# Attention and two expert layers on one core: cumulative logs moved to TensorE, k and q scaled by VectorE, the first expert's weights split during the last block, the last 512 tokens routed in one piece

## Chip, cores and metric

The kernel runs on one core of a Trainium2 chip. The metric is the device time of one execution in microseconds, median of several executions. Five engines work side by side, each through its own list of instructions in order: TensorE (PE, with PEld for its weight loads), VectorE (DVE), ScalarE (ACT), GpSimd (POOL), and SyncE (SP), which issues most transfers. An instruction waits for what it needs, and everything behind it on its engine waits too.

## Reference, cut to what matters

Three layers follow one another over 1536 tokens of 384 features.

```
for t in range(S):                       # gated linear attention, 2 x 8 heads, S=768, D=48
    state = f[t] * state + k[t] outer v[t]
    y[t] = q[t] @ state                  # f = sigmoid(f_logit)
h = x @ w_in                             # 384 -> 2048
g = h * tanh(softplus(h))
x = g @ w_out                            # 2048 -> 384
expert = argmax(x @ w_gate)              # 8 experts, up to 384 rows each, in token order
out = gate * (relu(x @ w1[e]) @ w2[e])   # 384 -> 1024 -> 384
```

## The kernel before

**Attention** is done in 12 chunks of 128 tokens (`chunk`). With c the running sum of log(1 + exp(-f_logit)) inside a chunk, k is multiplied by exp(c) and q by exp(-c), and matmuls do the rest. Steps of a chunk are named by its number: `e`, `l` (ACT, the logarithm), `sum` (DVE, the running sum, L575), `ek`, `eq` (ACT, the two exponentials, L582 and L585), `mk`, `mq` (POOL, the products, L589 and L591), `dd` (DVE, the chunk's whole decay, L593), `t`, `u`, `s`, `y` (PE: transposes of k, state update, scores, output), `sa` (DVE, the causal mask, L656), `d` (POOL, the decayed state, L637).

**The dense layer** goes in three blocks of 512 tokens and 16 groups of 128 hidden features: `H` (L757, 9 matmuls), the activation as a chain of ten instructions that alternate between ACT and DVE (L766, L773, L775, L770, L778, L780, L782, L784, L789, L792), and `A` (L801, 9 matmuls into three PSUM banks). Groups are counted 0 to 47, so H47 and A47 are the last. Products keep fp32 accuracy by splitting each operand into a high and a low part; the dense weights come packed and are decoded by ACT, DVE (L80, L82, L85) and POOL (L93) while the first block runs.

**Routing** (`copied`, `route`): after a block's last A the outputs are copied from PSUM (`xt`, L835, L837), logits taken (`lg`, L863), maximum and one-hot (`mx`, `oh`, L872, L877), positions counted (`pl`, `po`, L942 to L959), rows transposed (`tp`, L897) and scattered to DRAM. In the last block the first expert's rows do not go through DRAM: one-hot columns (`sel`, L982) and the split rows (`rh`, `rl`, L913, L915) go into matmuls (`mm`, L989) that add to the rows of earlier blocks (`d0`, L1017); their copies `0dh`, `0dl` are the input of expert 0.

**Experts** (`expert`, `expert_group`): each expert's weights are loaded in four pieces of 128 x 1536 and split by ACT and DVE in halves (`hi`, `lo`, L1064, L1066); expert 0 uses the memory of the dense layer's w_in, expert 1 that of w_out. Four hidden groups `EH` (L1147) and their second products `EA` (L1166) per expert follow; `tp`, `dh`, `dl` prepare the next expert's rows.

What runs when is decided by `Plan`: each step has an engine, a cost, a due time in units of groups and the steps it needs; a list scheduler turns that into one order, which is then fixed.

Of the kernel before, what the change touches and what calls it, by code (L numbers as in the profile page):

```python
# [34 lines left out]
class Kernel:  # L35
# [92 lines left out]
    def attention_scan(self, xg):  # L128
# [3 lines left out]
        with ExitStack() as ctx:  # L132
# [14 lines left out]
            for b in range(B):  # L147
                for g in range(H // 2):
                    tt = {}
                    for nm, src in (("q", self.q), ("k", self.k), ("f", self.f)):  # L150
                        t = tt[nm] = ld.tile([G, S], F32, tag="t" + nm, name="t" + nm)
                        for h in range(2):
                            nc.sync.dma_start(
                                out=t[h * D : (h + 1) * D, :].rearrange("p (c t) -> p c t", c=NC),
                                in_=src[b * NC : (b + 1) * NC, 64 * h : 64 * h + D, g, :].rearrange("c p t -> p c t"))
                    t = tt["f"]
# [255 lines left out]
class Plan:  # L412
# [4 lines left out]
    LAG = 80  # L417

# [9 lines left out]
    def order(self):  # L428
# [19 lines left out]
        while any(waiting.values()):  # L448
            for eng, w in waiting.items():
                if free[eng] > now:  # L450
                    continue
                for i, (_, _, s) in enumerate(w):
                    if not over(s["after"], now):
# [30 lines left out]
class Fast:  # L484
# [35 lines left out]
    def attention_setup(self):  # L520
        nc, pool = self.nc, self.work
        self.seg = pool.tile([128, H // 2, 128], F32, name="seg")
        nc.gpsimd.memset(self.seg, 1.0)
        nc.gpsimd.memset(self.seg[:, :, 0:1], 0.0)
# [16 lines left out]
    def chunk(self, n):  # L541
# [31 lines left out]
        def sums(_):  # L573
            T["cp"] = self.chunk_tile("cp", [128, H // 2, 128])
            nc.vector.tensor_tensor_scan(  # L575
                out=flat(T["cp"]), data0=flat(self.seg), data1=flat(T["f"]), initial=0.0, op0=ALU.mult, op1=ALU.add)
# [779 lines left out]
```

## Time and profile before

| | us |
|---|---|
| median of 3 executions | 497.9 (495.66 to 498.37) |
| the profiled execution: its own time | 500.67 |
| its span, first to last instruction | 498.9 |
| PE busy | 440.3 (88%) |
| DVE busy | 355.6 (71%) |
| ACT busy | 300.9 (60%) |
| POOL busy | 123.2 (25%) |
| mean granted TensorE clock (share of full) | 0.922 |

The busy share is a mean over stages that are limited by different engines, so the rows below are read by stage. An instruction's recorded time includes what it waits for after it has been started.

### The profile page before, as it was taken

How to read it: one execution, taken by the hardware profiler on the slowest of the kernel's cores; microseconds unless marked ns; L12 is line 12 of the kernel's file. 1: busy time of each engine (PE TensorE's matmuls, PEld its weight loads, DVE VectorE, ACT ScalarE, POOL GpSimd, SP SyncE). 2: the span in 40 equal slices, each digit the busy share in tenths (PEclk: the TensorE clock that was granted, in tenths of full speed). 3: DMA queues.
4: the chain of work that ended last, by engine and by line, in shares of the span. 5: the costliest groups of instructions: out<-in, count | busy, mean ns of one | idle time of the engine just before them, and what ended most of it. 6: DMA issues, size and time to landing. Idle time of an engine off the chain costs nothing.

```text
span 498.9 us, 7241 instructions
## 1 busy us (share of the span) xinstructions
PE 440.3 (88%) x2637; PEld 387.5 (78%) x2637; DVE 355.6 (71%) x590; ACT 300.9 (60%) x534; POOL 123.2 (25%) x114
## 2 busy tenths in 40 slices
PE   2964988894989999999999999577999999999992
PEld 2853776673768888888888888466999999999992
DVE  3889888999999975767787677976265475665310
ACT  5566587766577765557777777862274465556220
POOL 5688723325434221100001100004010121011011
PEclk9985778898999999999999999766899999999997
DMA  8765634444732001000600100464444865671000
GB/s 294 255 221 195 214 101 125 142 160 148 244 104 72 11 33 28 21 2 14 255 1 33 63 1 0 136 239 141 151 150 161 310 213 192 212 259 69 1 30 31
DMA packets 22047, 62.77 MB, mean 126 GB/s; under 512 B 3044, under 2 KB 10108, under 8 KB 22000
## 3 DMA queue, kind: packets, MB, share of 16 engines
q1 hardware_dynamic: 20208, 57.47, 34.7%
q0 software_dynamic: 1792, 4.73, 2.5%
q8 instruction: 23, 0.38, 0.3%
q14 instruction: 24, 0.20, 0.1%
HBM read 53.11 MB, written 8.68 MB: 124 GB/s over the span
## 4 chain that ended last, share of the span: by engine, by line
PE 41%; issue 28%; DVE 17%; DMA 6%; ACT 3%; POOL 2%; SPq 1%; POOLq 0%; DVEq 0%; ACTq 0%
PE bxp L801 16%; PE bhp L757 15%; DMA out_dram<-ys,rows 3%; DVE dec_t L85 3%; PE bat L670 2%; PE bat L675 2%; DVE dec_t L82 2%; PE bat L616 2%; PE bat L863 2%; DVE m_y L775 2%; PE bat L650 1%; DVE c_cp L575 1%; DVE dec_t L80 1%; DVE m_y L780 1%; DVE m_y L782 1%
## 5 line engine op out<-in xcount | busy, mean ns | idle before, releaser
L757 PE MATMUL bhp<-x,winh 128*128 128x512 f32 x288 | 90.9, 397 | 0.0
L757 PEld LDWEIGHTS bhp<-x,winh 128*128 128x128 f32 x288 | 54.1, 191 | 11.8 <-issue 0.6
L1156 DVE SCALAR_TENSOR_TENSOR gl<-bhp,gh 128x512 fp32r<-128x512 f32 x32 | 22.1, 690 | 56.9 <-ACT gh L1153 56.9
L1153 ACT ACTIVATE gh<-bhp 128x512 fp32r<-128x512 f32 x32 | 19.2, 600 | 66.2 <-PE bhp L1147 65.6
L757 PE MATMUL bhp<-x,winl 128*128 128x512 f32 x144 | 56.4, 392 | 0.0
L801 PE MATMUL bxp<-gh,wouth 128*128 128x512 f32 x144 | 45.7, 428 | 9.6 <-ACT gh L789 9.6
L1122 POOL DMA_INDIRECT out_dram<-ys,rows x16 | 16.4, 1024 | 127.6 <-ACT ys L1119 125.1
L969 POOL DMA_INDIRECT disp<-row,r_slot x12 | 14.5, 1208 | 131.6 <-ACT wouth L1064 58.0
L766 ACT ACTIVATE m_y<-bhp 128x512 f32<-128x512 f32 x48 | 28.6, 596 | 30.0 <-PE bhp L757 29.9
L801 PE MATMUL bxp<-gh,woutl 128*128 128x512 f32 x144 | 43.6, 413 | 0.0
L801 PE MATMUL bxp<-gl,wouth 128*128 128x512 f32 x144 | 43.4, 412 | 0.0
L780 DVE TENSOR_TENSOR m_y<-m_y,m_r 128x512 f32<-128x512 f32 x48 | 33.5, 699 | 11.4 <-ACT m_r L778 11.2
L770 ACT ACTIVATE m_r<-m_y 128x512 f32<-128x512 f32 x48 | 30.2, 630 | 17.2 <-DVE m_y L775 17.0
L792 DVE TENSOR_TENSOR gl<-bhp,gh 128x512 fp32r<-128x512 f32 x48 | 32.9, 686 | 9.8 <-ACT gh L789 9.3
L801 PEld LDWEIGHTS bxp<-gh,wouth 128*128 128x128 f32 x144 | 26.6, 199 | 16.7 <-ACT gh L789 11.8
L789 ACT ACTIVATE gh<-bhp 128x512 fp32r<-128x512 f32 x48 | 28.5, 594 | 13.6 <-DVE bhp L784 13.6
L782 DVE SCALAR_TENSOR_TENSOR m_y<-m_y,m_r 128x512 f32<-128x512 f32 x48 | 35.8, 748 | 0.8
L775 DVE TENSOR_SCALAR m_y<-m_y 128x512 f32<-128x512 f32 x48 | 26.0, 542 | 14.0 <-ACT m_y L773 13.6
L773 ACT ACTIVATE m_y<-m_y,root 128x512 f32<-128x512 f32 x48 | 34.7, 722 | 0.9
L801 PEld LDWEIGHTS bxp<-gl,wouth 128*128 128x128 f32 x144 | 29.0, 202 | 6.6
L801 PEld LDWEIGHTS bxp<-gh,woutl 128*128 128x128 f32 x144 | 28.9, 201 | 6.6
L1066 DVE TENSOR_TENSOR woutl<-raw,wouth 128x768 fp32r<-128x768 f32 x32 | 29.1, 953 | 6.5 <-ACT wouth L1064 6.3
(153 smaller groups left out, 1094.8 us busy)
## 6 DMA issues: line engine op xcount, KB each, us to landing
raw<-in_moe_w_dram SPq DMA_DIRECT2D x32, 768.0 KB, 5.1
stage<-in_moe_w_in_dram SPq DMA_DIRECT2D x8, 768.0 KB, 4.8
stage<-in_moe_w_out_dram SPq DMA_DIRECT2D x8, 768.0 KB
rows<-disp SPq DMA_DIRECT2D x9, 386.0 KB, 3.3
disp<-slot SPq DMA_DIRECT2D x1, 3088.0 KB, 11.1
c_f<-in_f_logit_dram SPq DMA_DIRECT2D x12, 256.0 KB, 3.9
c_k<-in_k_dram SPq DMA_DIRECT2D x12, 256.0 KB, 4.5
c_q<-in_q_dram SPq DMA_DIRECT2D x12, 256.0 KB, 3.7
```

The costliest lines, as they stand in the source:

```text
L757: nc.tensor.matmul(out=hp, lhsT=K.win[w][:, f // 2, kk, c], rhs=x[:, p, kk, :], start=(kk == 0 and n == 0), stop=(kk == KD - 1 and n == 2))
L766: nc.scalar.activation(out=T["y"], in_=T["h"], func=AF.Exp)
L770: nc.scalar.activation(out=T["r"], in_=T["y"], func=AF.Ln)
L773: add(f"{G}y2", "ACT", 740, G + .35, lambda _: nc.scalar.activation(out=T["y"], in_=T["y"], func=AF.Square, scale=ROOT, bias=K.root), [f"{ ...
L775: add(f"{G}y3", "DVE", 460, G + .4, lambda _: nc.vector.tensor_scalar(out=T["y"], in0=T["y"], scalar1=W_MAX, scalar2=0.5, op0=ALU.min, op1 ...
L780: add(f"{G}q1", "DVE", 740, G + .6, lambda _: nc.vector.tensor_tensor(out=T["y"], in0=T["y"], in1=T["r"], op=ALU.mult), [f"{G}r2"])
L782: add(f"{G}q2", "DVE", 740, G + .65, lambda _: nc.vector.scalar_tensor_tensor(out=T["y"], in0=T["y"], scalar=2.0, in1=T["r"], op0=ALU.subt ...
L789: nc.scalar.activation(out=T["g"][0], in_=T["h"], func=AF.Copy)
L792: add(f"{G}gl", "DVE", 700, G + .9, lambda _: nc.vector.tensor_tensor(out=T["g"][1], in0=T["h"], in1=T["g"][0].bitcast(F32), op=ALU.subtra ...
L801: nc.tensor.matmul(out=self.xa[kk][:, o], lhsT=K.wout[w][:, f, 128 * kk : 128 * (kk + 1)], rhs=T["g"][i][:, o], start=(f == 0 and n == 0), ...
L1066: nc.vector.tensor_tensor(out=lo[:, d], in0=r[:, s], in1=hi[:, d].bitcast(F32), op=ALU.subtract)
L1156: nc.vector.scalar_tensor_tensor(out=T["g"][1], in0=T["h"], scalar=0.0, in1=T["g"][0].bitcast(F32), op0=ALU.max, op1=ALU.subtract)
```

## The change

1. The running sum of a chunk is made by four matmuls with the causal matrix (`sum`, PE) instead of a scan on DVE. For that f_logit comes with tokens on the partitions. `ek`, `eq` and `dd` read it from PSUM; `dd` becomes an exponential on ACT.
2. `mk` and `mq` are done by DVE instead of POOL.
3. Expert 0's weights are split one half at a time when each part of w_in has been used for the last time, so during the last block. The last pieces wait for the activation of group 47. Expert 1's pieces wait until expert 0's rows are ready. The A of the last five groups is due one group later.
4. In the last block the four pieces of 128 tokens are routed together: one set of small instructions instead of two, with the row splits, gate weights and counts placed behind the one-hot columns.
5. `tp` of the experts is due later (u - .8 instead of u - 1.5), and the final check moves behind hidden group 2 of the experts.

```
-        add(f"{n}sum", "DVE", 700, u - 1, sums, [f"{n}l"], [(("cp",), [f"{n}mk", f"{n}mq", f"{n}dd"])])
+        def sums(taken):
+            T["lp"] = self.bank(taken[0])
+            for p in range(H // 2):
+                nc.tensor.matmul(
+                    out=T["lp"][:, 128 * p : 128 * (p + 1)], lhsT=T["f"][:, p, :], rhs=self.causal, start=True, stop=True)
+        add(f"{n}sum", "PE", 1050, u - 1, sums, [f"{n}l"], [(short[0], [f"{n}dd", f"{n}eq"])])
...
+        add(f"{n}dd", "ACT", 180, u - .75, whole, [f"{n}ek"])
-        add(f"{n}mk", "POOL", 1400, u - .6, lambda _: nc.gpsimd.tensor_tensor(
+        add(f"{n}mk", "DVE", 720, u - .6, lambda _: nc.vector.tensor_tensor(
             out=T["k"], in0=T["k"], in1=T["ek"], op=ALU.mult), [f"{n}ek", f"{n}k"])
-        add(f"{n}mq", "POOL", 1400, u - .5, lambda _: nc.gpsimd.tensor_tensor(
+        add(f"{n}mq", "DVE", 720, u - .5, lambda _: nc.vector.tensor_tensor(
             out=T["q"], in0=T["q"], in1=T["cp"], op=ALU.mult), [f"{n}eq", f"{n}q"])
...
-            add(f"A{G}{h}", "PE", 2040 if h == "" else 1080, G + self.LATE.get(h, 1.9), lambda _, o=o: across(_, o),
+            add(f"A{G}{h}", "PE", 2040 if h == "" else 1080, G + self.LATE.get(h, 2.1) + (G >= self.NG - 5), lambda _, o=o: across(_, o),
...
-        add(f"r{i}pl", "PE", 500, u + .1, place, [f"r{i}oh"] + ([f"r{i - 1}se"] if i else []), [(short, [f"r{i}po"])])
-        add(f"r{i}se", "DVE", 320, u + .2, seen, [f"r{i}pl"])
+        add(f"r{i}pl", "PE", 300 * count, u + .04, place, [f"r{i}oh"] + ([f"r{i - 1}se"] if i else []), [(short, [f"r{i}po"])])
+        add(f"r{i}se", "DVE", 160 * count, u + .4, seen, [f"r{i}pl"] + behind)
...
+        first = self.NG - NFB
+        def old(j):
+            G = first + 2 * j + 1
+            if e == 0:
+                return [f"H{G}"]
...
-            v = u - 4.5 + m + (.6 if m > 1 else 0)
+            v = u - 4.5 + m + (.6 if m > 1 else 0) if e else first + 4 * m + 4
...
+                add(f"{e}hi{m}{c}", "ACT", 850, v, lambda _, m=m, c=c: piece(m, c, True), [f"{e}raw{m}"] + old(2 * m + c) + (
+                    [f"0dl{KD - 1}"] if e == 1 else [f"{self.NG - 1}gl"] if e == 0 and m == 3 else []))
...
-                add(f"{e}tp{kk}", "PE", 260, u - 1.5, lambda taken, kk=kk: disp(kk, taken), [f"{e}rows"],
+                add(f"{e}tp{kk}", "PE", 260, u - .8, lambda taken, kk=kk: disp(kk, taken), [f"{e}rows"],
...
+        self.route(2 * self.NB - 2, self.NB - 1, 0, self.CPB, self.NG + .7, ("at", "xp0", "xp1", "xp2"))
```

Where the instructions stand is shown at three places, all on VectorE. First, the start of the program, from the first instruction of chunk 0; before the change:

```order
L575 SCALAR_TENSOR_TENSOR c_cp<-seg,c_f 128x512
L593 COPY dd<-c_cp 128x4
L575 SCALAR_TENSOR_TENSOR c_cp<-seg,c_f 128x512
L622 TENSOR_TENSOR c_st<-state_127,bat 128x384
L593 COPY dd<-c_cp 128x4
L656 TENSOR_TENSOR c_sa<-bat,causal 128x512
L656 TENSOR_TENSOR c_sa<-bhp,causal 128x512
```

The same place after it (L602 is `mk`, L604 `mq`, L667 the mask, L633 the state):

```order
L602 TENSOR_TENSOR c_k<-c_k,c_ek 128x512
L604 TENSOR_TENSOR c_q<-c_q,c_cp 128x512
L602 TENSOR_TENSOR c_k<-c_k,c_ek 128x512
L667 TENSOR_TENSOR c_sa<-bhp,causal 128x512 x2
L633 TENSOR_TENSOR c_st<-state_124,bhp 128x384
L604 TENSOR_TENSOR c_q<-c_q,c_cp 128x512
```

A scan and a small copy per chunk have gone; two products per chunk have come.

Second, VectorE while group 42 is in its activation, after the change (L786 to L803 are the activation, L1094 is the low half of a weight piece):

```order
L803 TENSOR_TENSOR gl<-bhp,gh 128x512
L791 TENSOR_TENSOR m_y<-m_y,m_r 128x512
L786 TENSOR_SCALAR m_y<-m_y 128x512
L793 SCALAR_TENSOR_TENSOR m_y<-m_y,m_r 128x512
L795 SCALAR_TENSOR_TENSOR bhp<-m_y,bhp 128x512
L791 TENSOR_TENSOR m_y<-m_y,m_r 128x512
L803 TENSOR_TENSOR gl<-bhp,gh 128x512
L793 SCALAR_TENSOR_TENSOR m_y<-m_y,m_r 128x512
L1094 TENSOR_TENSOR winl<-raw_2179,winh 128x768
L795 SCALAR_TENSOR_TENSOR bhp<-m_y,bhp 128x512
```

Six of the eight pieces now stand among the activations of groups 32 to 42 and two behind that of group 47; before, the first of the eight stood in that of group 46.

Third, VectorE from the copies of the last block's outputs on; before the change (L1066 is expert 1's weight split, L872 `mx`, L877 `oh`, L915 `rl`, L958 and L959 `po`):

```order
L835 COPY xt<-bxp_2317 128x256
L1066 TENSOR_TENSOR woutl<-raw_2866,wouth 128x768 x2
L872 TENSOR_REDUCE r_mx<-bat 128x2
L1066 TENSOR_TENSOR woutl<-raw_2883,wouth 128x768
L877 TENSOR_TENSOR r_oh<-bat,r_mx 128x16
L915 TENSOR_TENSOR rowl<-bat,rowh 128x384
L882 TENSOR_TENSOR r_ex<-bat,r_mx 128x16
L1066 TENSOR_TENSOR woutl<-raw_2883,wouth 128x768
L931 TENSOR_REDUCE r_sm<-r_ex 128x2
L932 TENSOR_SCALAR r_sm<-r_sm 128x2
```

After it (L897 `mx`, L902 `oh`, L941 `rl`, L986 and L987 `po`, L1012 `sel`):

```order
L855 COPY xt<-bxp_2360 128x256
L897 TENSOR_REDUCE r_mx<-bat 128x4
L902 TENSOR_TENSOR r_oh<-bat,r_mx 128x32
L941 TENSOR_TENSOR rowl<-bat,rowh 128x384
L941 TENSOR_TENSOR rowl<-bxp_2981,rowh 128x384
L941 TENSOR_TENSOR rowl<-bxp_2991,rowh 128x384
L986 TENSOR_TENSOR r_po<-r_oh,bxp_2996 128x32
L987 TENSOR_REDUCE r_slot_3023<-r_po 128x4
L1012 TENSOR_SCALAR sel<-iota_93,r_slot_3023 128x256
L941 TENSOR_TENSOR rowl<-bxp_3017,rowh 128x384
```

No weight piece stands in the routing any more, and there is one pass over four pieces of 128 tokens where there were two over two.

## Rows read from the trace of the kernel before

**Rows 1.** Three stages: engine busy us (instructions), granted clock, DMA share, GB/s

```profile
0.00:145.00 145.00, 108.26 (x633) 88.59 (x633) 128.34 (x172) 93.14 (x167) 77.90 (x68) 0.86 0.57 188
145.00:312.00 167.00, 165.95 (x892) 137.17 (x893) 127.50 (x248) 116.84 (x212) 23.03 (x26) 0.99 0.12 41
312.00:357.00 45.00, 33.13 (x169) 29.07 (x168) 30.10 (x73) 22.72 (x42) 5.84 (x5) 0.70 0.55 183
```

**Rows 2.** Groups by line, whole span: count | busy us, mean ns | idle before, releaser

```profile
L575 DVE TENSOR_TENSOR_SCAN c_cp<-seg,c_f 128x512 f32<-128x512 f32 x12 | 20.3, 1699 | 3.0 <-ACT c_f L568 3.0
L593 DVE COPY dd<-c_cp 128x4 f32<-128x4 f32 x12 | 4.9, 406 | 2.0 <-ACT c_cp L585 2.0
L85 DVE SCALAR_TENSOR_TENSOR dec_t<-stage,dec_t 128x768 int32<-128x768 int32 x16 | 22.0, 1376 | 0.0
L775 DVE TENSOR_SCALAR m_y<-m_y 128x512 f32<-128x512 f32 x48 | 26.0, 542 | 14.0 <-ACT m_y L773 13.6
L589 POOL TENSOR_TENSOR c_k<-c_k,c_ek 128x512 f32<-128x512 f32 x12 | 17.8, 1484 | 21.0 <-ACT c_ek L582 14.1 <-DVE m_y L782 3.5 <-DVE gl L792 2.9
L591 POOL TENSOR_TENSOR c_q<-c_q,c_cp 128x512 f32<-128x512 f32 x12 | 17.1, 1423 | 2.3 <-ACT c_cp L585 2.2
```

**Rows 3.** The same lines alone: duration ns min/median/max, first and last start

```profile
L575 DVE TENSOR_TENSOR_SCAN c_cp<-seg,c_f x12: 1208/1221/2868, 5.5 to 162.6; 128x512 f32<-128x512 f32 x12
L85 DVE SCALAR_TENSOR_TENSOR dec_t<-stage,dec_t x16: 944/954/2375, 17.4 to 139.6; 128x768 int32<-128x768 int32 x16
L775 DVE TENSOR_SCALAR m_y<-m_y x48: 412/427/2101, 60.8 to 316.1; 128x512 f32<-128x512 f32 x48
L780 DVE TENSOR_TENSOR m_y<-m_y,m_r x48: 674/684/1347, 64.6 to 319.7; 128x512 f32<-128x512 f32 x48
L784 DVE SCALAR_TENSOR_TENSOR bhp<-m_y,bhp x48: 668/690/697, 67.0 to 322.6; 128x512 f32<-128x512 f32 x48
```

**Rows 4.** What PE waited for, 20 to 145 us: total, times, longest

```profile
PE bat L600 <- POOL c_k L589: 7.3, 1, 7.3
```

**Rows 5.** The chain that ended last: start, us, what (slow and full clock)

```profile
52.73 2.05 PE bat L670 x8
227.00 0.89 PE bat L670 x8
```

**Rows 6.** Timeline of the dense layer's end: start, us, instruction, idle before

```profile
304.71 0.39 PE L757 MATMUL bhp<-x,winl 128*128 128x512 f32 x1
...
311.67 0.60 ACT L789 ACTIVATE gh<-bhp 128x512 fp32r<-128x512 f32 x1
...
312.87 0.39 PE L757 MATMUL bhp<-x,winl 128*128 128x512 f32 x1
...
323.99 1.65 PE L801 MATMUL bxp<-gh,wouth 128*128 128x512 f32 x3 [3.29 <-ACT gh L789]
...
326.71 1.48 PE L801 MATMUL bxp<-gl,wouth 128*128 128x512 f32 x3
```

**Rows 7.** What PE waited for, 312 to 360 us

```profile
PE bxp L801 <- ACT gh L789: 5.2, 2, 3.3
```

**Rows 8.** Timeline of the last block's routing up to expert 0

```profile
328.85 1.40 PE L863 MATMUL bat<-wg,xt 128*128 128x8 f32 x12
...
330.88 0.17 DVE L872 TENSOR_REDUCE r_mx<-bat 128x2 f32<-128x16 f32 x1
330.96 0.95 DVE L1066 TENSOR_TENSOR woutl<-raw,wouth 128x768 fp32r<-128x768 f32 x1
...
338.09 1.63 PE L989 MATMUL bhp<-sel,rowh 128*128 128x256 f32 x6
...
344.89 1.02 PE L989 MATMUL bhp<-sel,rowl 128*128 128x256 f32 x6
...
347.25 1.01 PE L1147 MATMUL bhp<-d,winh 128*128 128x256 f32 x3
```

**Rows 9.** Group by line: copy of an expert's rows on DVE

```profile
L1103 DVE TENSOR_TENSOR d<-bat,d 128x256 fp32r<-128x256 f32 x14 | 5.3, 415 | 0.0
```

More of the change, by code (lines that the diff above doesn't have):

```diff
@@ L451, in order @@
                     continue
+                soon = 1 << 60
                 for i, (_, _, s) in enumerate(w):
-                    if not over(s["after"], now):
+                    at = max([0] + [done.get(x, 1 << 60) for x in s["after"]])
+                    if at > now:
+                        soon = min(soon, at)
+                        continue
+                    if soon - now < self.PATIENCE * s["weight"]:
                         continue
@@ L852, in route @@
         last = b == self.NB - 1
         T = {}
-        u = NFB * (b + 1) + (1.5 + 3 * p if not last else .7 + p * .2)
-        xs = [f"{b}xt{kk}{p}" for kk in range(KD)]
-        short = ("at",) if not last else ("at", "hp")
-        def logits(taken):
-            lg = self.bank(taken[0])
-            for t in range(2):
-                o = 256 * p + 128 * t
+        ch = slice(p, p + count)
+        R = range(count)
+        small = lambda *x: self.route_small(b, *x)[:, ch]
+        behind = [f"r{i}sel{count - 1}"] if last else []
@@ L862, in logits @@
+        half = lambda t: [f"{b}xt{kk}{(p + t) // 2}" for kk in range(KD)]
+        def logits(t, taken):
+            if t == 0:
+                T["lgb"] = self.bank(taken[0])
+                T["lg"] = T["lgb"][:, : count * E].rearrange("p (t e) -> p t e", e=E)
+            for j in (t, t + 1):
+                o = 128 * (p + j)
                 for kk in range(KD):
                     nc.tensor.matmul(
-                        out=lg[:, E * t : E * (t + 1)], lhsT=self.xt[b][:, kk, o : o + 128],
+                        out=T["lg"][:, j], lhsT=self.xt[b][:, kk, o : o + 128],
@@ L915, in parts @@
                 nc.vector.tensor_tensor(out=T["rl"][:, t], in0=y, in1=T["rh"][:, t].bitcast(F32), op=ALU.subtract)
-        for t in range(2):
+        for t in R:
             ends = [f"r{i}row{t}"] + ([f"r{i}rl{t}"] if last else [])
-            add(f"r{i}tp{t}", "PE", 350, u + (.5 + .5 * t if not last else .05), lambda taken, t=t: rows(t, taken), xs + (
-                [f"r{i}tp0"] if t else []),
-                [(short, ends)] + ([(("row0" if b == 0 else "row",), [f"r{i}sc"])] if t == 0 else []))
+            add(f"r{i}tp{t}", "PE", 350, u + (.5 + .5 * t if not last else .05), lambda taken, t=t: rows(t, taken),
+                half(t) + ([f"r{i}tp{t - 1}"] if t else []) + ([f"r{i}pl"] if t == 3 else []),
+                [(short, ends)] + ([(("row0" if b == 0 else "row",), [f"r{i}sc{t // 2}"])] if t % 2 == 0 else []))
```

190 lines of the change are left out of this document (100 added, 90 removed).

## Prediction

> **What bounds the kernel now.** I read the busy time by stage first, because the share over the whole span (PE 88%) hides that three engines take turns. In the first 145 us VectorE is busy 128.3 us and PE only 108.3, at a granted clock of 0.86; from 145 to 312 PE is busy 166.0 of 167 us and nothing else matters; from 312 to 357 PE is busy 33.1 of 45 us at 0.70 of its clock [rows 1]. So a gain has to come out of VectorE before 145, and out of the waits between 312 and 357; in between, each microsecond put on PE is a microsecond lost.
>
> Next I asked why VectorE is so busy early. For single lines the view shows a median close to the minimum and a mean far above it: the scan 1221 ns median, 2868 at most, 1699 on average; the last decode step 954, 2375 and 1376; the clamp in the activation 427, 2101 and 542 [rows 2, 3]. The line L784, whose second input lies in PSUM, never goes beyond 697 ns [rows 3]. The excess of mean over median is 12 x 0.48 = 5.7 us for the scan, 16 x 0.42 = 6.8 for the decode step, 48 x 0.115 = 5.5 for the clamp: 18 us of VectorE's time in three lines is waiting, and almost all before 170 us, where GpSimd is busy 77.9 of 145 us [rows 1]. The products of k and q are 17.8 + 17.1 = 34.9 us of GpSimd's time [rows 2].
>
> By a rule of the Trainium skill ("SBUF — State Buffer", section "Who interferes with whom") a VectorE instruction with two SBUF inputs, or in a mode that uses both ports, and a GpSimd instruction that reads SBUF shut each other out for a whole instruction. The lines above agree. It also speaks against this change, see the second rival.
>
> Last the end of the dense layer. H45 ends at 305.10 and its high part `gh` at 312.27, so the activation takes 7.2 us up to the point where A can start. H47 ends at 313.26, but A47 starts only at 323.99 and ends at 328.19 [rows 6]: 10.7 us instead of 7.2, because expert 0's weight pieces stand between its instructions. PE waits for it twice, 5.2 us in all [rows 7]. From A47's end to expert 0's first matmul at 347.25 another 19.1 us pass; in them a weight piece of 0.95 us stands directly behind the first small routing instruction, and logits and matmuls run in two rounds [rows 8].
>
> **The change part by part.**
>
> *Scan, products and decay, up to 145 us.* VectorE loses 12 scans (20.3 us) and 12 small copies (4.9) [rows 2] and gets 24 products. The trace has no such product on VectorE; the nearest row is L780, the same shape with two SBUF inputs, at 684 ns [rows 3]: 16.4 us. Balance -8.8 us. On what stays, the waiting behind GpSimd should fall as GpSimd's work falls: 34.9 us go, nearly all of them early, out of some 85 to 90 that lie in the first 170 us (77.9 up to 145 [rows 1]), about 40%. Of the 12.3 us of excess in the decode step and the clamp that is -4.9. The new products will themselves wait sometimes: between 0 and what each scan waited, 24 x 0.48 = 11.5 us; L780's mean lies near its median, so I take 2. VectorE: -8.8 - 4.9 + 2 = about -12 us, bounds +3 (no relief, full waits) and -21 (all waits gone).
>
> How much of it reaches the end? PE has 36.7 us idle in this stage [rows 1] and must take the sums in. A sum is four matmuls of the shape of L670, whose eight records take 0.89 us at the upper clock level (2.4 GHz) and 2.05 us at the lower (1.2 GHz) [rows 5]. In the new order eight sums stand before group 12, some 8 to 16 us, hidden in idle time that is largely the very waiting for VectorE; one 7.3 us wait of PE for a product on GpSimd should go as well [rows 4]. PE gets tight, so I let 10 of the 12 us through: **-10** (bounds -18 and +3).
>
> *Four later sums.* They stand where PE is full: 4 x 0.89 = **+3.6**.
>
> *Expert 0's weights in the last block.* Six pieces of 0.95 us on VectorE [rows 8] and as many copies on ScalarE go among the activations of groups 32 to 42. Their cover is idle time: VectorE 127.5 and ScalarE 116.8 us busy of 167 [rows 1]. But latency counts too: `gh` of group 45 was ready 0.83 us before its A could start (312.27 against 313.10, the end of A44 and H47 as PE counts it) [rows 6]. A piece on each engine delays by up to 1.8 us, 1 us more than the slack. Bounds 0 and 6 x 1; I take **+1.5**.
>
> *End of the dense layer.* H47 comes one A earlier, since A44 to A47 stand behind it: -2.04, the time of an A as of an H (305.10 to 313.26 holds two of each). Without the pieces A47 can start 7.2 us after H47; three A fill 6.1 of them. It ends at about 7.2 + 2.3 = 9.5 us after H47, before it was 14.9: -5.4. What is late next is the copy of the outputs, not expert 0's weights: the two last pieces run beside A47. Together **-7.4** (bounds -9 and -5).
>
> *Routing in one piece.* From A47's end: copies up to the start of the logits 0.7 us (328.19 to 328.85); logits 1.4, one set of transposes 0.4 (three twelfths of the logits' 1.4), logits 1.4; maximum and one-hot, two of 0.17, 0.4 with their gaps; then PE's transposes and counts against VectorE's three row splits, which I put at 2.2 (three of three quarters of L780's 0.69, and 0.6 until the first can start); position and one `sel` 0.7, four times 0.17; 24 matmuls at the old 1.0 to 1.6 us for six, 5.2; and 1.3 from the last of them (345.91) to expert 0. That makes 13.7 against 19.1 us [rows 3, 8]. **-5.5** (bounds -8 at the upper clock, -3).
>
> *Expert 1's weights and the later `tp`.* Expert 1's pieces move out of the routing into expert 0, where VectorE is less than half busy; before the change the pieces of the following experts run there too. The next expert's row copies now have only two second products in front of them as cover, and in VectorE's order three pieces of 0.95 us stand among three copies of 0.42 [rows 8, 9]: 4.1 us against two products of about that length. **+0.5** (bounds 0 and 7 x 0.5).
>
> Sum: -10 + 3.6 + 1.5 - 7.4 - 5.5 + 0.5 = -17.3 us. The profiled execution took 500.67 us, its span 498.9; it would take 483.4. The median of the runs shown is 2.8 us lower, so I predict **480.5 us**.
>
> **The rivals.**
>
> *The early gain passes whole.* VectorE sheds its waits nearly completely and PE, less interrupted, keeps the upper clock: -18 in place of -10, 472.5 us. For it: PE's clock of 0.86 and 0.70 is low where it idles. Against: PE's extra sums in the same stage.
>
> *The products wait as the scans did.* GpSimd keeps the decode's low halves and the state updates; if every product waits 0.48 us and nothing else is relieved, VectorE gains nothing and the early term is 0: 490.5 us. By that rule of the Trainium skill each product, with two SBUF inputs, is exposed. Against: L780 has the same operands and a mean near its median, though most of it runs after GpSimd is done.
>
> *Routing gains half.* The chain of PE, ScalarE and VectorE in one piece has fewer overlaps than two rounds, and the clock stays low: -2.5 in place of -5.5, A47 -5 in place of -7.4: 486 us.
>
> *Slower.* PE takes its list in order, and a sum waits for ScalarE's logarithm; where that is late, groups queue behind it, as they did behind L600 for 7.3 us [rows 4]. There are 12 sums. To end more than 0.5% above the old time this would have to cost 17.3 + 2.5 = 19.8 us, or 1.65 us for each sum. Three waits like the one seen would do it. Against: PE has other work in front of most sums, and the logarithms are due a group ahead.
>
> **How the numbers follow.** The forecast with its own spread (476 to 485): 0.45. Whole early gain: 0.2. Waiting products: 0.15. Half the routing: 0.13. Slower: 0.03. The rest, 0.04, is a gain so small that it can't be told from none; about 0.5% is what a measurement of this kernel can tell. The range reaches from the better rival less 5 us (its bound of -21 us for VectorE and -8 for routing) to the waiting products: 467 to 491. Faster by over 0.5% (below 495.4) holds in all but the last two cases: 0.93; within 0.04; slower 0.03.
>
> **What would show it.** Right: the busy time of PE up to the point where it runs full shrinks in stretch, that point moves from 145 to 135 us or less, medians and means of the decode and clamp lines come together, the products stand near 0.69 us, from H47's end to expert 0's first matmul 23 us or less pass instead of 34. Wrong: the products show means near 1.2 us; PE waits for the logarithm in front of L580, or for `gh` in groups 33 to 43; PE waits for row copies between experts, which would show as idle time of up to 0.5 us before the first hidden group of each expert.

## Result and profile after the change

The changed kernel takes 482.2 us (479.68 to 483.49, 4 runs) where the kernel before takes 497.9 in the same comparison: ratio 0.969, 95% interval 0.964 to 0.974. A second comparison (below) gave 481.5 us and 0.965 (0.961 to 0.969). The profiled execution has a span of 480.5 us (before 498.9) and a mean granted clock of 0.951 (0.922). For one version below, "A later everywhere", time and ratio are from the four fast ones of its six executions, while its profile is of a slow one (492.5 us).

By stage, to be held against [rows 1]. The values are the stretch, its length, the busy us of PE, PEld, DVE, ACT and POOL (with instructions), the granted clock, the DMA share and GB/s. The first cut is where PE runs full; the last stretch holds more of the dense layer and of the experts than 312 to 357 us did before, so it is not the same work:

```profile
0.00:140.00 140.00, 112.62 (x704) 93.53 (x705) 117.08 (x172) 91.87 (x175) 47.04 (x48) 0.89 0.60 193
140.00:298.00 158.00, 157.68 (x875) 130.52 (x875) 120.36 (x241) 112.50 (x211) 14.61 (x20) 1.00 0.18 59
298.00:345.00 47.00, 44.41 (x263) 39.33 (x262) 32.35 (x65) 27.88 (x51) 4.63 (x4) 0.89 0.26 86
```

PE runs full from 140 us on (before: 146). Up to that point VectorE is busy 117.1 us in 172 instructions instead of 129.3 in 174 (before, cut at 146), PE 112.6 instead of 108.3, GpSimd 47.0 instead of 78.1.

The lines that waited behind GpSimd, and the new product, each alone (duration in ns, min/median/max), for [rows 3]:

```profile
L85 DVE SCALAR_TENSOR_TENSOR dec_t<-stage,dec_t x16: 940/945/1260, 20.8 to 134.8; 128x768 int32<-128x768 int32 x16
L786 DVE TENSOR_SCALAR m_y<-m_y x48: 408/426/1502, 57.6 to 309.7; 128x512 f32<-128x512 f32 x48
L602 DVE TENSOR_TENSOR c_k<-c_k,c_ek x12: 676/684/1626, 9.5 to 209.4; 128x512 f32<-128x512 f32 x12
```

and grouped over the whole span (busy us, mean ns), with the product of q (L604), for [rows 2]:

```profile
L786 DVE TENSOR_SCALAR m_y<-m_y 128x512 f32<-128x512 f32 x48 | 22.2, 462 | 9.6 <-ACT m_y L784 9.2
L85 DVE SCALAR_TENSOR_TENSOR dec_t<-stage,dec_t 128x768 int32<-128x768 int32 x16 | 15.4, 965 | 0.0
L604 DVE TENSOR_TENSOR c_q<-c_q,c_cp 128x512 f32<-128x512 f32 x12 | 9.8, 819 | 1.2 <-ACT c_cp L591 1.2
L602 DVE TENSOR_TENSOR c_k<-c_k,c_ek 128x512 f32<-128x512 f32 x12 | 9.4, 787 | 8.4 <-ACT c_ek L587 8.4
```

The mean of the decode step went from 1376 to 965 ns and now lies near its median of 945; the clamp's from 542 to 462, with a median of 426. The products take 787 and 819 ns on average, the one of k with a median of 684.

What PE waited for from 145 to 300 us, where the weight pieces of expert 0 now stand:

```profile
PE bxp L812 <- ACT gh L800: 0.3, 2, 0.2
```

The end of the dense layer and the routing, PE's timeline (L768 H, L812 A, L887 logits, L1018 `mm`, L1185 expert 0), for [rows 6, 8]:

```profile
307.02 0.39 PE L768 MATMUL bhp<-x,winl 128*128 128x512 f32 x1
...
314.84 0.96 PE L812 MATMUL bxp<-gh,wouth 128*128 128x512 f32 x3 [1.14 <-ACT gh L800]
...
316.33 0.86 PE L812 MATMUL bxp<-gl,wouth 128*128 128x512 f32 x3
317.02 0.82 PE L1046 MATMUL bhp<-ident,rows 128*128 128x128 f32 x6
317.68 1.40 PE L887 MATMUL bat<-wg,xt 128*128 128x8 f32 x12
...
324.12 1.01 PE L1018 MATMUL bhp<-sel,rowh 128*128 128x256 f32 x3
...
330.74 0.62 PE L1185 MATMUL bhp<-d,winh 128*128 128x256 f32 x3 [0.50 <-DVE d L1060]
```

H47 ends at 307.41, A47 starts 7.4 us later and ends at 317.19, expert 0 starts at 330.74: 23.3 us after H47 instead of 34.0. The nine matmuls of A47 stand in three lines of three (triples below). They take 0.96, 0.85 and 0.86 us where they took 1.65, 1.48 and 1.48 [rows 6]; the granted clock from A47's start to its end is 1.00 (2.4 GHz), before it was 0.50 (1.2 GHz). Before, PE waited 1.9 us ahead of A46 and 3.3 ahead of A47, and the lower level set in within A46; in the changed kernel PE waits once, 1.1 us. A46 before the change:

```profile
317.24 0.96 PE L801 MATMUL bxp<-gh,wouth 128*128 128x512 f32 x3 [1.94 <-ACT gh L789]
318.04 1.39 PE L801 MATMUL bxp<-gh,woutl 128*128 128x512 f32 x3
319.22 1.49 PE L801 MATMUL bxp<-gl,wouth 128*128 128x512 f32 x3
```

### The profile page after: what moved, and what is told of

Read it like the earlier page. It is cut to its first block, busy times and chain, and to the rows that moved or that the text cites. A ratio compares the mean times of both kernels' runs of the same rounds, so it can differ in the third digit from the quotient of the medians.

```text
span 480.5 us, 7381 instructions
## 1 busy us (share of the span) xinstructions
PE 441.4 (92%) x2737; PEld 389.4 (81%) x2737; DVE 339.8 (71%) x582; ACT 298.2 (62%) x545; POOL 87.5 (18%) x88
## 4 chain that ended last, share of the span: by engine, by line
PE 44%; issue 26%; DVE 13%; DMA 9%; ACT 5%; SPq 1%; POOL 1%; POOLq 0%; DVEq 0%; ACTq 0%
PE bxp L812 15%; PE bhp L768 15%; DMA out_dram<-ys,rows 4%; DVE m_y L791 2%; DVE m_y L793 2%; PE bat L661 2%; PE bat L627 2%; PE bat L681 2%; DMA disp<-row,r_slot 2%; PE bat L580 2%; DVE bhp L795 2%; PE bat L887 2%; PE bat L686 1%; DVE dec_t L82 1%; DVE dec_t L85 1%
## 5 line engine op out<-in xcount | busy, mean ns | idle before, releaser
L768 PE MATMUL bhp<-x,winh 128*128 128x512 f32 x288 | 91.9, 401 | 2.8 <-DMA x<-c_y 2.8
L768 PEld LDWEIGHTS bhp<-x,winh 128*128 128x128 f32 x288 | 53.2, 190 | 15.5 <-DMA c_f<-in_f_logit_dram 2.5
L768 PE MATMUL bhp<-x,winl 128*128 128x512 f32 x144 | 56.7, 394 | 0.0
L812 PE MATMUL bxp<-gh,wouth 128*128 128x512 f32 x144 | 44.5, 418 | 8.6 <-ACT gh L800 8.6
L791 DVE TENSOR_TENSOR m_y<-m_y,m_r 128x512 f32<-128x512 f32 x48 | 35.8, 746 | 13.8 <-ACT m_r L789 13.6
L1160 POOL DMA_INDIRECT out_dram<-ys,rows x16 | 21.2, 1327 | 117.6 <-ACT ys L1157 115.1
L812 PE MATMUL bxp<-gh,woutl 128*128 128x512 f32 x144 | 41.9, 400 | 0.0
L812 PE MATMUL bxp<-gl,wouth 128*128 128x512 f32 x144 | 41.2, 395 | 0.0
L803 DVE TENSOR_TENSOR gl<-bhp,gh 128x512 fp32r<-128x512 f32 x48 | 33.0, 687 | 8.8 <-ACT gh L800 8.0
L812 PEld LDWEIGHTS bxp<-gh,wouth 128*128 128x128 f32 x144 | 25.9, 194 | 16.1 <-ACT gh L800 11.0
L800 ACT ACTIVATE gh<-bhp 128x512 fp32r<-128x512 f32 x48 | 28.5, 593 | 15.0 <-DVE bhp L795 14.9
L781 ACT ACTIVATE m_r<-m_y 128x512 f32<-128x512 f32 x48 | 30.0, 628 | 12.3 <-DVE m_y L786 12.1
L997 POOL DMA_INDIRECT disp<-row,r_slot x12 | 13.6, 1136 | 130.4 <-DVE row L961 56.5
L795 DVE SCALAR_TENSOR_TENSOR bhp<-m_y,bhp 128x512 f32<-128x512 f32 x48 | 33.0, 687 | 0.3
L812 PEld LDWEIGHTS bxp<-gh,woutl 128*128 128x128 f32 x144 | 27.9, 194 | 6.3
L812 PEld LDWEIGHTS bxp<-gl,wouth 128*128 128x128 f32 x144 | 27.6, 192 | 6.1
L768 PEld LDWEIGHTS bhp<-x,winl 128*128 128x128 f32 x144 | 27.3, 190 | 6.0
```

Of the source, the lines that this page charges most:

```text
L768: nc.tensor.matmul(out=hp, lhsT=K.win[w][:, f // 2, kk, c], rhs=x[:, p, kk, :], start=(kk == 0 and n == 0), stop=(kk == KD - 1 and n == 2))
L781: nc.scalar.activation(out=T["r"], in_=T["y"], func=AF.Ln)
L791: add(f"{G}q1", "DVE", 740, G + .6, lambda _: nc.vector.tensor_tensor(out=T["y"], in0=T["y"], in1=T["r"], op=ALU.mult), [f"{G}r2"])
L795: add(f"{G}q3", "DVE", 700, G + .7, lambda _: nc.vector.scalar_tensor_tensor(out=T["h"], in0=T["y"], scalar=1.0, in1=T["h"], op0=ALU.add, ...
L800: nc.scalar.activation(out=T["g"][0], in_=T["h"], func=AF.Copy)
L803: add(f"{G}gl", "DVE", 700, G + .9, lambda _: nc.vector.tensor_tensor(out=T["g"][1], in0=T["h"], in1=T["g"][0].bitcast(F32), op=ALU.subtra ...
```

## Experiments

All kernels at a glance. The ratio is to the kernel before, run beside each of them; the other columns come from one profiled execution each.

| kernel | us | ratio (95%) | H47 ends | A47's end behind it | from there to expert 0 | from there to the span's end |
|---|---|---|---|---|---|---|
| before | 498.8 | 1 | 313.26 | 14.9 | 19.1 | 151.7 |
| changed | 482.2 | 0.969 (0.964 to 0.974) | 307.41 | 9.8 | 13.6 | 149.8 |
| changed, again | 481.5 | 0.965 (0.961 to 0.969) | 308.94 | 9.8 | 13.5 | 149.9 |
| attention part alone | 495.4 | 0.992 (0.989 to 0.995) | 308.13 | 14.9 | 19.0 | 149.5 |
| all but the attention part | 483.7 | 0.969 (0.965 to 0.973) | 310.46 | 9.8 | 11.9 | 149.9 |
| products on GpSimd | 483.4 | 0.968 (0.963 to 0.972) | 311.83 | 9.8 | 12.9 | 149.8 |
| before, products on VectorE | 496.8 | 0.996 (0.993 to 0.999) | 310.01 | 14.5 | 18.9 | 151.2 |
| two routing pieces | 480.0 | 0.964 (0.960 to 0.968) | 304.48 | 9.8 | 11.0 | 152.3 |
| expert 0's weights late | 486.3 | 0.975 (0.972 to 0.979) | 304.80 | 15.5 | 12.8 | 150.5 |
| products mixed | 488.4 | 0.979 (0.975 to 0.982) | 311.82 | 10.1 | 13.0 | 151.4 |
| A later everywhere | 488.6 | 0.978 (0.973 to 0.983) | 318.87 | 9.0 | 12.9 | 149.9 |
| two pieces, weights not held | 483.6 | 0.970 (0.965 to 0.974) | 306.31 | 9.8 | 14.5 | 150.2 |
| two pieces, few banks | 484.3 | 0.972 (0.969 to 0.975) | 306.81 | 9.9 | 14.5 | 149.7 |
| two pieces, routing as before | 485.0 | 0.972 (0.969 to 0.975) | 306.83 | 9.8 | 16.8 | 149.9 |

**The two halves of the change.** First the attention part alone (the edits to `sum`, `ek`, `dd`, `eq`, `mk`, `mq` and the layout of f_logit, on the kernel before), then everything else alone.

> The attention part of the change alone (sums on TensorE, decay on ScalarE, products on VectorE), everything behind it as before. By the prediction's sum its two terms give -10 + 3.6 = -6.4 us: about 491.5 us where before has 497.9, VectorE's busy time up to the point where PE runs full falls by about 10 us and that point lies at 137 or earlier. Rival one, the products wait as the scans did: 0 + 3.6, about 501 us. Rival two, the early gain passes whole: -18 + 3.6, about 483.5 us.

> All of the change but the attention part: expert 0's weights split in the last block, one A later near the end, the last 512 tokens routed in one piece, the later row copies. The prediction's terms for it are +1.5 - 7.4 - 5.5 + 0.5 = -10.9 us: about 487 us, with some 23 us from the end of H47 to expert 0's first matmul instead of 34. Rival: the two parts lean on each other (a VectorE that is busy with scans and waits delays the pieces in groups 32 to 42, or the pieces cost nothing), then alone it gives less than 8 us (490 or more) or more than 13 (485 or less), and the two parts' gains don't add up to the 15.6 us measured for both.

The attention part alone gives -3.9 us (0.79% of 498.8; -5.5 to -2.3), less than the -6.4 forecast. The rest alone gives -15.6 (-17.6 to -13.7), more than the -10.9 and beyond the 13 us at which its rival begins. That the whole came out within 2 us of the forecast is luck: the two errors cancel. The parts' sum, -19.5, is above what both together give (-15.5 and -17.4 in the two comparisons); with intervals of 2 us on each that is not settled as an overlap. Where the rest alone gained more than forecast is seen in its profile (the table's rows, against before): -2.8 us up to H47 (forecast -2.04 + 1.5 = -0.5; a time that scatters by some 4 us, see the end), -5.1 to A47's end (-5.4), -7.2 from there to expert 0 (-5.5), -1.8 in the experts (+0.5). In the profile the attention part lowers VectorE's busy time by about what was expected, from 129.3 to 117.5 us, but brings PE's full point only to 140 and not to the 137 or earlier that were expected:

```profile
0.00:140.00 140.00, 112.99 (x707) 93.95 (x708) 117.50 (x172) 92.64 (x175) 47.29 (x48) 0.89 0.58 193
```

**Products back on GpSimd, and products alone moved.**

```
-        add(f"{n}mk", "DVE", 720, u - .6, lambda _: nc.vector.tensor_tensor(
+        add(f"{n}mk", "POOL", 1400, u - .6, lambda _: nc.gpsimd.tensor_tensor(
```

and the same for `mq`, on the changed kernel; the reverse edit on the kernel before.

> The changed kernel with the products of k and q back on GpSimd; the sums stay on TensorE. Theory, the waiting behind GpSimd is what VectorE got rid of: the means of the last decode step and of the clamp rise again towards 1.38 and 0.54 us with minima unchanged, PE waits for products, and the time is about 4 us above the changed kernel's 482.2. Rival, VectorE's own work is what bounds the early stage: it is rid of 24 products, 16 us, and the kernel takes 480 us or less with the point where PE runs full at 136 or earlier.

> The kernel before with nothing changed but that the products of k and q run on VectorE; the scan and the small copies of the decay stay there. Theory, VectorE bounds the early stage and waits behind GpSimd: it gets 24 products of 0.69 us, 16.4 us, and sheds at most the excess of the scan, the decode step and the clamp, 10 to 18 us; so -2 to +6 us, taken +3: 501 us, with the scan's mean near its median of 1.22. Rival, the excess of those lines has nothing to do with GpSimd: means stay at 1.70, 1.38 and 0.54, and all 16.4 us are added, 510 us or more.

With the products back on GpSimd the time is 483.4 us, the changed kernel's within its interval. Neither side of the expectation fits: the decode step's mean rises only to 1053 ns, but the waiting moves to the two decode steps ahead of it. VectorE's groups up to 180 us in that kernel, and then the first two of them in the changed one:

```profile
L82 DVE SCALAR_TENSOR_TENSOR dec_t<-stage,dec_t 128x768 int32<-128x768 int32 x16 | 21.6, 1348 | 0.2
L80 DVE TENSOR_SCALAR dec_t<-dec_t 128x768 int32<-128x768 int32 x16 | 18.5, 1156 | 6.2 <-ACT dec_t L76 6.2
L85 DVE SCALAR_TENSOR_TENSOR dec_t<-stage,dec_t 128x768 int32<-128x768 int32 x16 | 16.8, 1053 | 0.1
```

```profile
L82 DVE SCALAR_TENSOR_TENSOR dec_t<-stage,dec_t 128x768 int32<-128x768 int32 x16 | 17.8, 1112 | 0.2
L80 DVE TENSOR_SCALAR dec_t<-dec_t 128x768 int32<-128x768 int32 x16 | 12.3, 766 | 0.0
```

The three decode lines together take 56.9 us with the products on GpSimd and 45.5 in the changed kernel; in the kernel before they take 54.1, and 44.9 there with the products moved. So GpSimd's products go with some 10 us on VectorE's decode lines, and still the total time of the two versions can't be told apart.

With the products alone moved, the time is 2.1 us lower (0.7 to 3.5), at the good end of the -2 to +6 expected; the rival (+16 us) is out. VectorE's groups up to 180 us in that one:

```profile
L85 DVE SCALAR_TENSOR_TENSOR dec_t<-stage,dec_t 128x768 int32<-128x768 int32 x16 | 16.8, 1052 | 0.0
L575 DVE TENSOR_TENSOR_SCAN c_cp<-seg,c_f 128x512 f32<-128x512 f32 x12 | 16.5, 1393 | 3.8 <-ACT c_f L568 3.8
L589 DVE TENSOR_TENSOR c_k<-c_k,c_ek 128x512 f32<-128x512 f32 x12 | 10.4, 870 | 0.7 <-ACT c_ek L582 0.7
```

Scan and decode step fall from 1699 and 1376 ns [rows 2] to 1393 and 1052 though neither was touched: 24 products left GpSimd's list and entered VectorE's. So most of their excess over the median went with GpSimd's products, about two thirds for the scan and three quarters for the decode step; the scan's mean did not come down to its median of 1.22 as expected, and GpSimd still has 86.9 us of other work. The new product waits too: 870 ns on average against a median of 682. The Trainium skill ("SBUF — State Buffer", section "Who interferes with whom") has a VectorE instruction with two SBUF inputs and a GpSimd instruction that reads SBUF shut each other out; these three means agree.

**Products by chunk, and A one group later everywhere.** Two attempts at a faster version of the early stage, on the changed kernel:

```
-        add(f"{n}mk", "DVE", 720, u - .6, lambda _: nc.vector.tensor_tensor(
+        pe, pn, pw = ("DVE", nc.vector, 720) if n < 4 else ("POOL", nc.gpsimd, 1400)
+        add(f"{n}mk", pe, pw, u - .6, lambda _: pn.tensor_tensor(
...
```

and the same for `mq`; and

```
-            add(f"A{G}{h}", "PE", 2040 if h == "" else 1080, G + self.LATE.get(h, 2.1) + (G >= self.NG - 5), lambda _, o=o: across(_, o),
+            add(f"A{G}{h}", "PE", 2040 if h == "" else 1080, G + self.LATE.get(h, 3.1), lambda _, o=o: across(_, o),
```

> The changed kernel with the products of the first four chunks on VectorE as in the change and those of the other eight on GpSimd. In the traces the changed kernel starts H0 at 49.4 us and the version with all products on GpSimd at 52.7, but the latter makes up for it from 60 to 140 us, where VectorE is full in the changed kernel. Theory, VectorE bounds the stretch from 60 to 140: both gains together, H0 at 49.5 and the point where PE runs full at 136 or earlier, the time 478 to 480. Rival, what bounds that stretch is PE with its attention work and the waits between the engines, and VectorE's work is nearly free there: 481 to 484.

> The changed kernel with every A one group later (3.1 groups behind its H), as only the last five are now. Early PE waits 7.2 us in three waits for gh in front of an A. Theory: with one more group between H and A these waits go, and PE runs full some 3 us earlier: 479 us. Rival: the time that PE stands there is set by VectorE, which has the same work to do; PE then waits for something else, and the time is the same as the changed kernel's, 481 to 484; or with all three buffers of gh in use a later A holds back the next activation, and it is slower.

Both are slower, by some 6 us each (ratios 0.979 and 0.978 against the changed kernel's 0.967, the mean of its two), so both theories fall, and the first one's rival with them; the second is slower as its last rival said. PE's longest wait up to 165 us in the mixed version, and in the version with the later A, in the profile of its 492.5 us execution:

```profile
PE bhp L769 <- DMA x<-c_y: 7.0, 1, 7.0
```

```profile
PE bhp L768 <- DVE gl L803: 14.4, 4, 6.3
```

The mixed version brings a block's inputs late, in a transfer behind the last chunk's split: 7.0 us where the changed kernel waits 2.4 at most for one. In the other, an H waits for one of the three banks that the activation has not yet set free; a wait of the activation for an A, as the rival had it, is not in that trace up to 165 us, so why this version is slower stays open. Taken together, the time does not follow the sum of VectorE's work in the early stage: with 24 products more on it the kernel before was 2.1 us faster, with 24 fewer the changed kernel was the same, with 16 fewer 6 us slower. That the length of the chain through a chunk or an activation decides instead is a reading of these waits and not shown.

**Expert 0's weights behind H47 again.** On the changed kernel, with the later A kept:

```
-            v = u - 4.5 + m + (.6 if m > 1 else 0) if e else first + 4 * m + 4
+            v = u - 4.5 + m + (.6 if m > 1 else 0)
...
-                return [f"H{G}"]
+                return [f"H{self.NG - 1}"]
```

> The changed kernel with expert 0's weight pieces moved back behind H47. Theory: the pieces stand between the activation's instructions again, A47 starts 10.7 us after H47 instead of 7.4, and its end comes some 3 us later; the 1.5 us taken for the pieces in groups 32 to 42 come back; in sum about +2 us, 484 us, without a wait for gh in groups 33 to 43. Rival one, the pieces in groups 32 to 42 cost nothing and behind H47 they also lengthen the routing: +5 us or more, 487 us. Rival two, the later A alone is what shortened the end: no difference.

It takes 486.3 us, 4 to 5 more than the changed kernel, between the theory and its first rival. PE's timeline at A47:

```profile
316.79 0.97 PE L812 MATMUL bxp<-gh,wouth 128*128 128x512 f32 x3 [3.92 <-ACT gh L800]
317.59 1.45 PE L812 MATMUL bxp<-gh,woutl 128*128 128x512 f32 x3
318.83 1.49 PE L812 MATMUL bxp<-gl,wouth 128*128 128x512 f32 x3
```

H47 ended at 304.80: A47 starts 12.0 us later instead of 7.4, and of its triples behind that wait of 3.9 us the second and third take 1.45 and 1.49 us, about as long as before the change (granted clock 0.62 over the three, where the changed kernel has 1.00). It ends 15.5 us after H47, 5.7 more than with the pieces spread. The later A alone is not what shortened the end.

**The routing: two pieces, weights held or not, more or fewer banks.** Four versions of the changed kernel with two pieces of 256 tokens. The first keeps the held-back weights and the five banks (the split rows and one-hot columns get two buffers, and the counts no longer wait for the last one-hot columns); the second gives expert 1's weights their old release; the third the old banks; the fourth both. The edits, cut to what matters:

```
-        self.route(2 * self.NB - 2, self.NB - 1, 0, self.CPB, self.NG + .7, ("at", "xp0", "xp1", "xp2"))
+        for h in range(2):
+            self.route(2 * self.NB - 2 + h, self.NB - 1, 2 * h, 2, self.NG + .7 + .2 * h, ("at", "xp0", "xp1", "xp2"))
```

```
-                return [f"A{G}{h}" for h in self.parts(G)]
+                return [f"A{self.NG - 1}{h}" for h in self.parts(self.NG - 1)]
...
-                    [f"0dl{KD - 1}"] if e == 1 else [f"{self.NG - 1}gl"] if e == 0 and m == 3 else []))
+                    [f"{self.NG - 1}gl"] if e == 0 and m == 3 else []))
```

```
-        self.route(2 * self.NB - 2, self.NB - 1, 0, self.CPB, self.NG + .7, ("at", "xp0", "xp1", "xp2"))
+        for h in range(2):
+            self.route(2 * self.NB - 2 + h, self.NB - 1, 2 * h, 2, self.NG + .7 + .2 * h, ("at", "hp"))
```

> The changed kernel with the last 512 tokens routed in two pieces of 256, each with its own logits, places and matmuls, and with expert 1's weight pieces still kept out of the routing. Theory, the number of rounds costs: from A47's end to expert 0's first matmul 18 to 19 us instead of 13.6, the time 5 to 6 us above the changed kernel: 487.5 us. Rival, what cost there before was the weight piece that stood directly behind the first small routing instruction: then two pieces without it take 15 us or less, and the time is 484 us or less.

> Two routing pieces as in the version that took 480.0 us, with its five banks, but expert 1's weight pieces released behind A47 as before the change, so that they stand among the small routing instructions again (two ahead of the first and second of them on VectorE). In that version 11.0 us pass from A47's end to expert 0's first matmul. Theory, these pieces are most of what made the old routing slow: 15 us or more, 484 us or more. Rival, the banks are: 12 us or less, the time unchanged at 480 to 481.

> Two routing pieces with expert 1's pieces held back, but with the banks of before: TensorE's results of the routing go only to the two banks of the ring at (the three of hp are taken by expert 0's rows), no longer also to the three that the dense layer's outputs leave free. Theory, the pieces of weights made the old routing slow: 12.5 us or less from A47's end to expert 0's first matmul, 482 us or less. Rival, the banks did, since each transpose has to wait until a row of the one before is split: 15 us or more, 484 us or more.

> Two pieces, expert 1's weights not held back and the banks of before: the old routing in full, all else as changed. Theory, pieces and banks together are the old routing's cost and one piece for two is worth nothing: 18 to 19 us from A47's end to expert 0's first matmul, about 488 us. Rival, half of it was the lower clock level into which PE had fallen before A47 in the kernel before, and which these versions reach later: 15 us or less, 484 us or less.

> The changed kernel as it is, for the comparison on one chip with the three that follow and for its scatter. Two profiles of kernels whose instructions stand in the same order up to group 32 showed H47's end at 304.5 and 304.8 us where the changed kernel's had 307.4. Theory, that is scatter from one execution to the next: this profile's H47 ends anywhere from 304 to 308, the median stays at 482 and the ratio within 0.964 to 0.974. Rival, the order at the end does act on the early stage: H47's end again within 0.5 us of 307.4.

The rival of the first one holds: two pieces take 11.0 us from A47's end to expert 0, one piece 11.9 to 13.6 in seven profiles: putting the rows together gained nothing that can be seen. PE's timeline with two pieces:

```profile
313.44 0.85 PE L812 MATMUL bxp<-gl,wouth 128*128 128x512 f32 x3
...
319.06 0.63 PE L1018 MATMUL bhp<-sel,rowh 128*128 128x256 f32 x3
...
322.76 0.62 PE L1018 MATMUL bhp<-sel,rowh 128*128 128x256 f32 x3 [1.81 <-DVE sel L1012]
...
325.33 1.01 PE L1185 MATMUL bhp<-d,winh 128*128 128x256 f32 x3 [0.50 <-DVE d L1060]
```

The first `mm` starts 4.8 us after A47's end instead of 6.9 (324.12 - 317.19): it needs the places of two pieces of 128 tokens and not of four. That pays for the second round and its wait of 1.8 us.

The clock has a part in these lengths. The stretch from A47's end to expert 0, in this order: the changed kernel, all but the attention part, two pieces, two pieces with weights not held, with few banks, with the routing as before:

```profile
317.19:330.74 13.55, 12.09 (x81) 11.04 (x79) 6.92 (x28) 5.58 (x15) 1.69 (x2) 0.62 0.21 72
320.29:332.14 11.85, 9.94 (x80) 9.10 (x79) 6.73 (x28) 5.50 (x15) 0.98 (x1) 0.86 0.19 69
314.29:325.33 11.04, 8.74 (x76) 7.94 (x74) 7.59 (x36) 5.52 (x16) 0.88 (x1) 0.93 0.19 73
316.11:330.60 14.49, 11.98 (x78) 11.09 (x75) 10.06 (x39) 10.24 (x21) 2.17 (x2) 0.65 0.33 116
316.66:331.11 14.45, 11.53 (x76) 10.64 (x74) 7.79 (x36) 5.58 (x16) 2.73 (x4) 0.76 0.23 83
316.64:333.41 16.77, 13.50 (x77) 12.02 (x75) 12.87 (x42) 10.84 (x23) 2.90 (x4) 0.59 0.52 168
```

In the first two VectorE and ScalarE have the same instructions in the same order, and yet the stretch takes 13.55 us at a granted clock of 0.62 and 11.85 at 0.86; four more versions with this routing lie between (0.71 to 0.74, 12.8 to 13.0). Two pieces had 0.93. So the 2.5 us between two pieces and the changed kernel are in part the clock, and the two can't be ranked by these profiles.

Released early, the weights add 3.5 us (14.5); with the old banks it is 3.4 (14.5); with both 5.7 (16.8, between what the theory and its rival gave). So each is about half of the old routing's excess, where I had expected one of them to be nearly all, and the two overlap in part. These prices include the clock: of them 3.2, 2.8 and 4.8 us are longer busy time of PE, at 0.65, 0.76 and 0.59 instead of 0.93, and only 0.2 to 1.0 us more idle time. Whether weights and banks brought the clock down was not tried. In total time, by the ratios, the three are 3, 4 and 4 us behind two pieces, with intervals of 2 us on each. VectorE's timeline with the weights not held shows them ahead of each of the first two small instructions:

```profile
317.46 0.95 DVE L1094 TENSOR_TENSOR woutl<-raw,wouth 128x768 fp32r<-128x768 f32 x1
318.32 0.17 DVE L897 TENSOR_REDUCE r_mx<-bat 128x2 f32<-128x16 f32 x1
318.41 0.95 DVE L1094 TENSOR_TENSOR woutl<-raw,wouth 128x768 fp32r<-128x768 f32 x1
319.27 0.17 DVE L902 TENSOR_TENSOR r_oh<-bat,r_mx 128x16 bf16<-128x16 f32 x1
```

and PE's waits with few banks, 300 to 345 us, show transposes (L922) that wait for the bank of an earlier step:

```profile
PE bat L922 <- DVE r_po L986: 1.1, 2, 0.8
PE bhp L1018 <- DVE seen L977: 1.0, 1, 1.0
```

The last 2.3 us up to the 19.1 of before were in none of these versions. The clock is hardly their reason: over that stretch it was 0.68 before and 0.59 in the version with 16.8 us. PE stood idle 6.6 us instead of 3.3. One thing there is seen in the trace of before and was not tried singly: the final check's small instructions stood on VectorE ahead of `0dl`, which is L1031, and PE waited 1.1 us for the check's result just ahead of expert 0:

```profile
345.93 0.15 DVE L1190 SCALAR_TENSOR_TENSOR count<-iota,bat 128x8 f32<-128x8 f32 x1
...
346.62 0.22 DVE L1204 TENSOR_REDUCE al<-ok 128x1 f32<-128x69 f32 x1
346.77 0.42 DVE L1031 TENSOR_TENSOR d<-bhp,d 128x256 fp32r<-128x256 f32 x1
```

```profile
347.00 0.19 PE L1208 MATMUL bat<-al 128*1 128x1 f32 x2 [1.09 <-DVE al L1205]
```

In total time the version with two pieces (0.960 to 0.968) and the changed kernel (0.961 to 0.969) can't be told apart; against two pieces with the old routing (0.969 to 0.975) it is 4 us ahead.

## Why the prediction came out right, step by step

The time, 480.5 us forecast, was met within 2 us, and the range held it. The steps fared unequally.

*Scan, products and decay (-10).* The size for VectorE was right: -12.3 up to the full point (129.3 to 117.1), forecast -12. That 10 of it reach the end was too much. PE's idle time up to that point did fall by 10 (146 - 108.3 = 37.7 to 140 - 112.6 = 27.4), but PE's busy time rose by 4.4. The failing step is the sentence that the sums are hidden in idle time: that idle time was itself the gain, and I counted it twice. The sums cost PE 12.2 us there (L580 by window: 4.12, 2.14, 2.39, 1.05, 1.05, 1.42). PE's waits for the product of k did go, from 16.2 us up to 165 us to 3.8. PE's full point came to 140, not to the 135 or less given as a sign of being right. With the later sums at +2.9, the -3.9 us of the attention part alone leaves -6.8 for this term; in the two profiles 5.1 us of the difference lie up to H47 and 2.2 in the experts, so the early share of the -3.9 may be smaller. On top of the rest of the change the part is worth 0 to 2 us by the medians, with 3 us of uncertainty.

*Four later sums (+3.6).* Near: one takes 1.05 us where 0.89 was taken, but three and not four run after 140 us, 1.81 + 1.05 = 2.9 us.

*Expert 0's weights in the last block (+1.5).* Too much: PE waits 0.3 us in all for `gh` from 145 to 300.

*End of the dense layer (-7.4).* Right where it can be read: A47's end lies 9.8 us behind H47 (forecast 9.5, before 14.9) in eight profiles with the pieces spread (10.1 with mixed products, 9.0 with A later everywhere), and 15.5 with the pieces put back. The 2.3 us that the sum took for A47 itself were met (2.35 instead of 4.20), but without a reason: they need the upper clock level behind the wait, and the prediction didn't say why it should hold there. The 2.04 us of the earlier H47 are hidden in the scatter of its time.

*Routing in one piece (-5.5).* The sum was right, 13.55 and 13.53 us against a forecast of 13.7, and its cause was not: the two rounds cost nothing that can be seen. Held-back weights and three more banks are worth 5.7 us in the profiles, the clock included, and some 4 in the total time; I had named the weights, left the banks out, and given the credit to the edit that the change is called by.

*Expert 1's weights and the later `tp` (+0.5).* No wait between experts, so 0 in place of +0.5. Instead the experts got 1.9 us shorter (151.7 to 149.8), a term that I did not have. Expert 0's first 4 us in windows (the third value from the end is the granted clock), before, after, with the attention part alone and with two pieces:

```profile
347.25:351.25 4.00, 4.00 (x18) 4.00 (x19) 0.79 (x3) 0.00 (x0) 0.91 (x1) 0.50 0.76 268
```

```profile
330.74:334.74 4.00, 4.00 (x33) 4.00 (x34) 3.81 (x6) 3.78 (x7) 2.58 (x3) 1.00 0.46 130
```

```profile
342.10:346.10 4.00, 4.00 (x33) 4.00 (x34) 1.48 (x4) 0.60 (x1) 0.90 (x1) 1.00 0.80 275
```

```profile
325.33:329.33 4.00, 4.00 (x18) 4.00 (x19) 3.31 (x5) 2.24 (x4) 2.43 (x3) 0.50 0.46 123
```

Of the 14 profiles of the table three begin the experts at the lower level (151.7, 152.3, and 151.2 for products alone moved on the kernel before) and eleven at the upper: 149.5 to 150.5, and 151.4 with mixed products, where PE waits 1.2 us inside. That the attention part alone, with nothing changed behind it, has 149.5 shows that this is not the later `tp`'s doing. What decides the level there was not tried.

Of the rivals, "the whole early gain passes" and "the products wait as the scans did" both fall at the attention part alone (-3.9, between -14.4 and +3.6). "Routing gains half" falls at the 13.6 us, though the clock did stay low as it said (0.62). "Sums wait for the logarithm" is seen once in the changed kernel, for 6.1 us in the first 20, and not in front of later groups. Of the other signs, PE's wait for `gh` in groups 33 to 43 is 0.3 us in all, and the products' means of 787 and 819 ns lie nearer to 0.69 us than to the 1.2 of a wrong prediction: 12 x 0.10 + 12 x 0.14 = 2.9 us of waiting, where 2 were taken.

## What to carry to other kernels

When work moves from a crowded engine to one that stands idle because of the crowding, the idle time can be spent once: either it is the gain or it is the cover. Before a latency-bound chain is merged into fewer, larger steps, look at what else stands between its instructions and which buffers it waits for; here holding back background work and more banks gave 5.7 us, the clock included, and the merge nothing that could be seen. Read the granted clock beside the length of a stretch before two versions are compared by it. And time the halves of a change by themselves: here the total came out right over two halves that were off by 2.5 and 4.7 us in opposite directions.

## What was not expected of the hardware

One and the same stage scatters more from execution to execution than the edits differ. In five versions whose instructions stand in the same order as the changed kernel's up to the second block's routing (the four with two pieces and the one with expert 0's weights late), and in the changed kernel twice, H47 ended between 304.5 and 308.9 us; the changed kernel's second profile, expected from 304 to 308 if this was scatter and at 307.4 if it was the order, had the 308.9, outside both. So one profile's early stage tells little about less than 4 us, while the way from H47's end to A47's end (9.78 to 9.85 us in eight profiles) repeats within 0.1. The routing behind it repeats only where the clock does: 13.55 and 13.53 us in the changed kernel at 0.62, but 11.9 at 0.86 with the same instructions. The time as a whole goes with the clock too. Of ten executions of the changed kernel, six had a mean granted clock of 0.950 or 0.951 and took 481.8 to 484.4 us, four had 0.969 and took 478.7 to 480.5; both its profiles are of the first group, and what sets the clock is not known.

The waiting between VectorE and GpSimd is not tied to a line. When VectorE's instructions shift against GpSimd's, it leaves one decode step and turns up in another (L85 1376 to 1053 ns, L82 1151 to 1348 and L80 859 to 1156 with the sums on PE and the products still on GpSimd); only its sum over lines is a price, 54.1 and 56.9 us with the products on GpSimd against 44.9 and 45.5 without.
